# First layer in blocks of 512 tokens with all its weights resident, areas laid out by phase, and the GpSimd differences on VectorE

## Chip, cores and metric

One NeuronCore of a Trainium2 chip runs the kernel. The metric is the device time of one execution in microseconds (us), median of several runs. Five engines run side by side, each in the order of its own queue: PE (TensorE, the matmuls), DVE (VectorE), ACT (ScalarE), POOL (GpSimd) and SP, which here only issues DMAs.

## What is computed

Linear attention with a normalisation per head, then two feed-forward layers, all in fp32:

```python
kv = einsum('bhsd,bhse->bhde', k, v)                   # 8 batches, 8 heads, 576 tokens, head size 64
out = einsum('bhsd,bhde->bhse', q, kv)
x = out / sqrt(mean(out * out, axis=-1) + 1e-6) * g_norm   # (4608 tokens, 512)
h = x @ w_in                                           # layer one: (512, 2048)
x = (maximum(h, 0) + alpha * minimum(h, 0)) @ w_out    # (2048, 512)
return ((x @ w_a) * (x @ w_b)) @ w_out2                # layer two: (512, 1536) twice, (1536, 512)
```

## The kernel before

**Precision and products.** Every operand of the layers is split into a rounded high half (fp32r) and the rest, and a product is three matmuls (high by low, low by high, high by high). Each large product uses Strassen's scheme in Winograd's form on 2 x 2 quarters: seven sub-products instead of eight, paid for with additions and differences of quarters before and after. A sub-product has two slices of 128 rows, so it is six matmuls.

**Units.** A unit is the weight operand of one 256-column piece: its seven combinations, both halves, in one of eight places `w0` to `w7`. Weights arrive as 64-bit words. `to_float` (L229) turns them into floats with one ACT, four DVE and one POOL operation (L237 to L244); `combine` (L448) forms the four combinations S1 to S4 (L454) and splits them (ACT L461, DVE L463). A unit is made in one of two ways. With `fetch` and `direct` it is made straight from the input, as six of the eight `w_in` units are. With `convert` and `build`, floats are first written to DRAM (`wd`) and later read back when a place is free; then the combinations of L454 run on POOL.

**Stages.** Attention is 16 steps (two a batch): products of k and v (L278, L279), q by that (L295, L300), the norm on ACT and DVE, the scaling by it on POOL (L339), a transposition on PE (L349, L353), and a store of the result to `xd` in DRAM. The first four steps run ahead; the other twelve are put between products of layer one, two steps a piece of work, behind the first six pieces. Layer one and two then each have a stage of first products (`first`, PE line L540) and of second products (`second`, L616).

In `first` a piece is one block of 768 tokens by one pair of units. `X` loads the block into the place F0 (L485), forms differences of its quarters (`less`, L500) and splits the seven operands into `rops` (ACT L507, DVE L508). The differences of the first block may run on DVE; those of all later blocks are on POOL. Each sub-product is 384 wide and has a bank of PSUM for each unit; ACT copies it to H (L547) or DVE adds it (L550). Then layer one's activation follows (ACT L577 and L578, DVE L579), or the product of a and b in layer two (L582), and H is stored to `gd` in DRAM. H alternates between the places F1 and F2.

In `second` a block is 512 tokens; for each of 8 (layer one) or 6 (layer two) units it loads 256-wide quarters of `gd` into one of the places F0, F1, F2 (L597), forms four differences (L602: the first on POOL, three on DVE), splits them (ACT L608, DVE L609) into one of three parts of `rops` and adds 42 matmuls to seven banks. After the last unit ACT copies one bank (L625) and DVE adds the others (L629).

**Order.** Nothing is ordered by hand. `Plan.add` records each operation with its cost, priority and data it reads and writes; `Plan.order` (L113) is a list scheduler that places them on engines by these costs, and its order is the program's order on every engine. An operation waits for the older users of a place that it overwrites.

Priorities are due times: START for the first piece, URGENT for copies and additions of banks, `due` for conversions. The list V (L658) gives the sequence of blocks; six places hold units until attention ends, two more come from the memory that attention frees.

Of the kernel before, what the change touches and what calls it, by code (L numbers as in the profile page):

```python
# [24 lines left out]
NB1, NB2 = TOK // T1ST, TOK // T2ND  # L25
CH = 112
EPS = 1e-6
QN = 2
# [6 lines left out]
PAIR = 14 * 6 * (N1 + 32) / 2400  # L35
UNIT2 = 7 * 6 * (N2 + 32) / 2400
START, STEP = 50.0, 12.5
ATT = 30.0
NFIRST = 4
BUILD, CONVERT = 14.0, 10.0  # L40
# [112 lines left out]
def body(ctx: ExitStack, tc, kvm, kvt, qt, gn, w_in, alpha, w_o1, w_a, w_b, w_o2, outT):  # L153
# [19 lines left out]
    def in_dram(shape, name):  # L173
        t = dram.tile(shape, F32, name=name)
        return Buf(lambda: t)
# [16 lines left out]
    rops = pool.tile([P, 7 * 4 * N1], F32R, name="rops")  # L192
# [17 lines left out]
    def bank(tag, shape):  # L210
        return place(tag, shape, F32, psum)

    tenants = []

    def rop(lo, n):

        before = []
        for e in list(tenants):
            a, z, b = e
            if a < lo + n and lo < z:  # L220
                before += b.tasks
                if lo <= a and z <= lo + n:
                    tenants.remove(e)
        b = Buf(lambda: rops[:, lo:lo + n], before)
        tenants.append((lo, lo + n, b))
        return b

# [25 lines left out]
    class Step:  # L253
# [57 lines left out]
        def norm(self):  # L311
# [6 lines left out]
            for s in range(2):  # L318
                sq = place("T1", [P, NT, P])
# [22 lines left out]
        def tr(self, tags):  # L342
# [11 lines left out]
            y = [sb("y", [P, SEQ], 3) for _ in range(2)]  # L354
# [17 lines left out]
    def slot(key, shape, dt):  # L372
        old = plan.rings.get(key)
        b = Buf(lambda: (late[0] if key in SLOTS[6:] else pool).tile(shape, dt, tag=key, name=key),
                old.tasks if old else (attention if key in SLOTS[6:] else ()))
# [3 lines left out]
    class Unit:  # L379
# [57 lines left out]
        def build(self, key, prio):  # L437
# [5 lines left out]
            self.combine(prio, 1, "p")  # L443
# [27 lines left out]
    class X:  # L471


        def __init__(self, la, b):
            self.la, self.b = la, b
            self.x = place("F0", [P, 4, 2, N1])

        def load(self, prio):
            xf, t0, done = self.x, self.b * T1ST, 0
            src, size = (x2d, T2ND) if self.la else (xd, SEQ)  # L480
            while done < T1ST:
                p, o = divmod(t0 + done, size)
                m = min(T1ST - done, size - o)
                hs = [h for h in range(2) if done < (h + 1) * N1 and done + m > h * N1]
                dma(m * 2048, lambda done=done, m=m: xf.t.rearrange("p k h t -> p k (h t)")[:, :, done:done + m],  # L485
                    lambda p=p, o=o, m=m: src[p].t[:, :, o:o + m], prio, [(src[p], k) for k in range(4)],
                    [(xf, (r, h)) for r in range(2) for h in hs])
                done += m

        def operands(self, prio, engines="v", split_on="v"):  # L490
# [349 lines left out]
```

## Time and profile before

| What | Value |
|---|---|
| median of 3 runs (lowest, highest) | 1813.35 us (1812.14, 1814.52) |
| the profiled execution's own time | 1813.78 us |
| its span, first to last instruction | 1812.0 us |
| PE, DVE, ACT, POOL busy in the span | 92%, 74%, 48%, 33% |
| mean granted clock of PE | 0.962 |
| moved by DMA | 287.10 MB, 158 GB/s |

A row of the stretches has, after its bounds and length, the busy time of each engine and its number of instructions, the granted clock of PE as a share of full speed, and DMA's share and rate. A row of a group has the line, engine and operation, what it writes and reads, the count, the busy time and mean duration (ns), then the idle time ahead of it and what ended that. A waiting row has the waiting engine and line, what it waited for, the total in us, the times and the longest. A row with three durations gives the least, the median and the greatest in ns. In a timeline, start and length in us stand first and an idle time ahead, with its cause, in brackets.

### The profile page before, as it was taken

How to read it: one execution, taken by the hardware profiler on the slowest of the kernel's cores; microseconds unless marked ns; L12 is line 12 of the kernel's file. 1: busy time of each engine (PE TensorE's matmuls, PEld its weight loads, DVE VectorE, ACT ScalarE, POOL GpSimd, SP SyncE). 2: the span in 40 equal slices, each digit the busy share in tenths (PEclk: the TensorE clock that was granted, in tenths of full speed). 3: DMA queues.
4: the chain of work that ended last, by engine and by line, in shares of the span. 5: the costliest groups of instructions: out<-in, count | busy, mean ns of one | idle time of the engine just before them, and what ended most of it. 6: DMA issues, size and time to landing. Idle time of an engine off the chain costs nothing.

```text
span 1812.0 us, 28663 instructions
## 1 busy us (share of the span) xinstructions
PE 1662.9 (92%) x11132; PEld 1636.3 (90%) x11132; DVE 1349.3 (74%) x1794; ACT 864.9 (48%) x1223; POOL 593.2 (33%) x423
## 2 busy tenths in 40 slices
PE   5588968879899699999998999999999999999998
PEld 5487868879799599999998999999999999999998
DVE  5886755788867789889898767666785557778785
ACT  4466756767678433333334543444544334333332
POOL 2323224332334223433345723223633112222221
PEclk8798978989899899999999999999999999999999
DMA  8646866454534445455554333334353223444442
GB/s 247 226 139 214 257 221 196 150 195 159 204 140 167 164 158 163 158 159 166 174 190 156 128 134 134 122 124 152 137 174 130 105 87 120 131 143 138 149 132 93
DMA packets 174440, 287.10 MB, mean 158 GB/s; under 512 B 14304, under 2 KB 95200, under 8 KB 174304
## 3 DMA queue, kind: packets, MB, share of 16 engines
q1 hardware_dynamic: 174304, 285.28, 47.4%
q8 instruction: 87, 1.43, 0.3%
q14 instruction: 49, 0.40, 0.1%
HBM read 176.17 MB, written 109.05 MB: 157 GB/s over the span
## 4 chain that ended last, share of the span: by engine, by line
PE 68%; DVE 15%; issue 7%; ACT 5%; POOL 3%; DMA 1%; SPq 0%; DVEq 0%; ACTq 0%; POOLq 0%
PE b L540 42%; PE b L616 21%; ACT rops L608 2%; PE b L295 2%; DVE F L602 2%; DVE rops L609 2%; DVE rops L508 2%; POOL stg L454 1%; DVE F L579 1%; PE b L278 1%; DVE stg L239 1%; DVE F L550 1%; DVE w L463 1%; PE b L349 1%; POOL stg L244 1%
## 5 line engine op out<-in xcount | busy, mean ns | idle before, releaser
L540 PE MATMUL b<-rops,w 128*128 128x384 f32 x5040 | 916.1, 342 | 65.1 <-DVE rops L508 33.4
L540 PEld LDWEIGHTS b<-rops,w 128*128 128x128 f32 x5040 | 890.0, 192 | 79.7 <-DVE rops L508 34.9
L616 PE MATMUL b<-rops,w 128*128 128x256 f32 x5292 | 644.6, 285 | 27.8 <-DVE rops L609 22.6
L616 PEld LDWEIGHTS b<-rops,w 128*128 128x128 f32 x5292 | 639.2, 192 | 33.3 <-DVE rops L609 23.8
L608 ACT CAST rops<-F 128x1792 fp32r<-128x1792 f32 x126 | 211.6, 1694 | 409.5 <-DVE F L602 131.9
L547 ACT COPY F<-b 128x384 f32<-128x384 f32 x480 | 228.1, 478 | 353.3 <-PE b L540 346.3
L609 DVE TENSOR_TENSOR rops<-F,rops 128x1792 fp32r<-128x1792 f32 x126 | 264.9, 2116 | 98.4 <-ACT rops L608 97.3
L550 DVE TENSOR_TENSOR F<-F,b 128x384 f32<-128x384 f32 x360 | 194.6, 549 | 179.4 <-ACT F L547 85.8
L602 POOL TENSOR_TENSOR F<-F 128x256 f32<-128x256 f32 x126 | 148.0, 1178 | 395.4 <-DMA F<-gd 334.9
L244 POOL TENSOR_TENSOR stg<-stg 128x512 f32<-128x512 f32 x56 | 100.2, 1789 | 314.2 <-DVE stg L242 170.1
L602 DVE TENSOR_TENSOR F<-F 128x256 f32<-128x256 f32 x378 | 180.2, 504 | 8.3 <-DMA F<-gd 4.0
L508 DVE TENSOR_TENSOR rops<-F,rops 128x768 fp32r<-128x768 f32 x120 | 148.7, 1253 | 19.9 <-ACT rops L507 19.6
L454 POOL TENSOR_TENSOR stg<-stg 128x256 f32<-128x256 f32 x112 | 123.5, 1114 | 66.3 <-DMA stg<-wd 55.1
L579 DVE SCALAR_TENSOR_TENSOR F<-F,nal_sb,t 128x768 f32<-128x768 f32 x96 | 117.3, 1233 | 32.7 <-ACT F L578 32.2
L507 ACT CAST rops<-F 128x768 fp32r<-128x768 f32 x120 | 98.6, 836 | 23.5 <-POOL F L500 11.1
L500 POOL TENSOR_TENSOR F<-F 128x768 f32<-128x768 f32 x38 | 77.5, 2044 | 55.1 <-DVE rops L508 54.3
L577 ACT ACTIVATE t<-F 128x768 f32<-128x768 f32 x96 | 80.9, 847 | 21.8 <-DVE F L579 19.6
L463 DVE TENSOR_TENSOR w<-stg,w 128x1792 fp32r<-128x1792 f32 (+2 forms) x36 | 76.7, 2134 | 18.2 <-ACT w L461 18.1
L582 DVE TENSOR_TENSOR F<-F 128x768 f32<-128x768 f32 x72 | 80.5, 1125 | 13.0 <-ACT F L547 12.4
L578 ACT ACTIVATE F<-F 128x768 f32<-128x768 f32 x96 | 79.8, 844 | 0.6
L339 POOL TENSOR_TENSOR o<-o,sm 128x640 f32<-128x640 f32 x32 | 48.9, 1548 | 92.1 <-DVE sm L334 87.8
L500 POOL TENSOR_TENSOR T<-F 128x768 f32<-128x768 f32 x19 | 38.0, 1998 | 123.5 <-DMA F<-x2d 77.4
(64 smaller groups left out, 883.7 us busy)
## 6 DMA issues: line engine op xcount, KB each, us to landing
gd<-F SPq DMA_DIRECT2D x168, 384.0 KB, 2.8
F<-gd SPq DMA_DIRECT2D x252, 256.0 KB, 3.0
kvm<-in_kvm_dram SPq DMA_DIRECT2D x32, 448.0 KB, 5.4
wd<-stg SPq DMA_DIRECT2D x56, 256.0 KB, 2.0
stg<-in_w_o_dram SPq DMA_DIRECT2D x28, 512.0 KB, 4.7
stg<-wd SPq DMA_DIRECT2D x56, 256.0 KB, 3.5
F<-x2d SPq DMA_DIRECT2D x12, 1024.0 KB, 6.3
q<-in_qt_dram SPq DMA_DIRECT2D x32, 288.0 KB, 3.3
```

The source lines that it names most:

```text
L244: task("p", n, lambda: nc.gpsimd.tensor_add(out(), permute(f32(a())), permute(f32(u()))), prio, [A, U], [dst])
L454: sub(256, lambda e, o=o, f=f, a=a, b=b: getattr(e, f)(c.t[:, o], c.t[:, a], c.t[:, b]), prio, r, [(c, {S1: "S1", S2: "S2", S3: "S3", S4: ...
L500: sub(n, lambda e: e.tensor_sub(o[0](), a[0](), b[0]()), prio, a[1] + b[1], o[1], engines)
L508: sub(n, lambda e: e.tensor_sub(w(1), v(), f32(w(0))), prio, a[1] + [(c, 0)], [(c, 1)], split_on)
L540: nc.tensor.matmul(bk.t[:, 0:N1], w.h.t[:, a, i, kk, :], ct[:, b, kk, :], start=bool(new and kk == 0 and m == 0), stop=(kk == 1 and m == 2 ...
L547: task("a", N1, lambda: nc.scalar.copy(H.t[:, u, q], bk.t[:, 0:N1]), t - URGENT, [(bk, 0)], [(H, (u, q))])
L550: task("v", N1, lambda: nc.vector.tensor_add(H.t[:, u, q], H.t[:, u, q], bk.t[:, 0:N1]), t - URGENT, [(bk, 0), (H, (u, q))], [(H, (u, q))])
L579: task("v3", T1ST, lambda r=r, v=v, nal=nal: nc.vector.scalar_tensor_tensor(v(), v(), nal, r.t, ALU.mult, ALU.add), t, pv + [(r, 0)], pv)
L602: sub(N2, lambda e, o=o, a=a, c=c: e.tensor_sub(s.t[:, o[0]], s.t[:, a[0]], s.t[:, c[0]]), k - 9, [a[1], c[1]], [o[1]], on)
L608: task("a", 7 * N2, lambda: nc.scalar.copy(half(0), s.t[:, 0:7]), k - 7, reads, [(c, 0)])
L609: sub(7 * N2, lambda e: e.tensor_sub(half(1), s.t[:, 0:7], f32(half(0))), k - 7, reads + [(c, 0)], [(c, 1)], "v")
L616: nc.tensor.matmul(bk[i].t[:, m], unit.h.t[:, a, i, m, :], half(e)[:, i], start=bool(j == 0 and m == 0 and z == 0), stop=bool(j == n - 1 a ...
```

## The change

- Blocks of `first` in layer one are 512 tokens (256-wide sub-products, nine blocks, 36 pieces instead of 24); layer two keeps 768.
- All eight `w_in` units are fetched and made directly in the eight places and stay until the last block of the stage; all blocks take the four pairs in turn.
- Attention steps after the fourth come one to two pieces; the first four have due times 0, 8, 30 and 40. q has three buffers instead of two.
- The copies and additions of banks take both units in one operation (512 elements in layer one, 768 in layer two). X, Y and Z are one bank each in layer one (X alternating between two), two banks each in layer two.
- Fixed places F0 to F2 give way to ranges of two areas, `fa` and `rops`, and of two more, `rl` and `fl`, that exist from the end of attention. `second` rotates over four source places instead of three.
- All differences of operands and of `second`, and the combinations in `build`, run on DVE; POOL keeps one addition of `to_float` (L244 before) and the scaling in attention.
- The due times of conversions are spread between the stages' needs, and the loads of blocks come earlier.

```diff
-T1ST, N1 = 768, 384
+T1ST = (512, 768)
-QN = 2
+QN = 3
-START, STEP = 50.0, 12.5
-ATT = 30.0
+START = 40.0
+ATT = 20.0
+STEP_AT = [0, 8, 30, 40]
+FETCH_AT = [4, 12, 20, 25, 32, 36, 42, 48]
-    rops = pool.tile([P, 7 * 4 * N1], F32R, name="rops")
+    rops = pool.tile([P, 7168], F32R, name="rops")
+    fa = pool.tile([P, 7680], F32, name="fa")
...
-            self.combine(prio, 1, "p")
+            self.combine(prio)
...
-    def first(k, la, units, js, x):
+    def first(k, la, units, js, x, odd):
+        t1st, n1, pair = T1ST[la], T1ST[la] // 2, PAIR[la]
+        places = [((0, 1), (6, 7))[odd], (2, 3), (4, 5)] if la else [odd, 2, 3]
+        X_, Y_, Z_ = [bank(i, [P, 2, 256]) for i in places]
+        H = area("f", odd * 8 * n1, 8 * n1, (2, 4, n1))
...
-        def copy(u, q, bk, t):
-            task("a", N1, lambda: nc.scalar.copy(H.t[:, u, q], bk.t[:, 0:N1]), t - URGENT, [(bk, 0)], [(H, (u, q))])
+        def copy(q, bk):
+            task("a", 2 * n1, lambda: nc.scalar.copy(H.t[:, :, q], bk.t[:, :, 0:n1]), k + pos * dt - URGENT,
+                 [(bk, 0), (bk, 1)], [(H, (0, q)), (H, (1, q))])
...
+        prod(0, X_, 1)
+        copy(0, X_)
+        prod(2, Y_, 1)
+        copy(3, Y_)
+        prod(1, X_, 0)
+        copy(1, X_)
+        prod(4, Z_, 1)
+        add(0, Z_)
+        prod(3, X_, 0)
+        add(3, X_)
+        prod(5, Y_, 0)
+        add(1, Y_)
+        prod(6, X_, 0)
+        copy(2, X_)
...
+    SOURCE = [[("f", 4096), ("fl", 0), ("f", 0), ("f", 2048)], [("fl", 0), ("f", 0), ("f", 4096), ("f", 2048)]]
+    TURN = [[2, 0, 1], [0, 1, 2]]
...
-        for o, a, c, on in ((t3, b22, b12, "p"), (t1, b12, b11, "v"), (t2, b22, t1, "v"), (t4, b21, t2, "v")):
+        for o, a, c, on in ((t3, b22, b12, "v"), (t1, b12, b11, "v"), (t2, b22, t1, "v"), (t4, b21, t2, "v")):
-        c = rop((plan.counts.setdefault("gx", 0) % 3) * 14 * N2, 14 * N2)
+        c = rop(TURN[la][(b * n + j) % 3], 14 * N2)
...
-    V = [(0, 0, [0, 1, 2]), (0, 1, [0, 1, 2]), (0, 2, [0, 1, 2, 3]), (0, 0, [3]), (0, 3, [0, 1, 2, 3]), (0, 1, [3]),
-         (0, 4, [0, 1, 2, 3]), (0, 5, [0, 1, 2, 3])]
+    V = [(0, b, [0, 1, 2, 3]) for b in range(NB1[0])]
...
-            x.load(tn - 30)
-            x.operands(tn - 9, "p", "pv")
+            x.load(tn - 70)
+            x.operands(tn - 9)
```

PE's order around the later attention steps, before (L540 are products of layer one, L349 and L353 transpose a step, L295 and L300 are q's products of the next, L278 and L279 the k and v products of the one after):

```order
L540 MATMUL b_2120<-rops,w_530 128x384 x6
L349 MATMUL b_2131<-ident,o_109 128x112 x4
L295 MATMUL b_2139<-kvbd,q_2073 112x128 x4
L349 MATMUL b_2146<-ident,o_109 128x112 x4
L353 MATMUL b_2152<-ident,o_109 128x128 x2
L295 MATMUL b_2158<-kvbd,q_2079 112x128 x4
L300 MATMUL b_2164<-kvbd,q_2073 128x128
L300 MATMUL b_2164<-kvbd,q_2079 128x128
L278 MATMUL b_2171<-kvm_2092 128x128 x4
L279 MATMUL b_2171<-kvt_2100 128x128
L278 MATMUL b_2171<-kvm_2103 128x128 x4
L279 MATMUL b_2171<-kvt_2110 128x128
```

The next step's own matmuls follow these rows, again with no product between. At the like place of the changed kernel (L576 are its products, L380 and L384 the transposition of one step):

```order
L380 MATMUL banks<-ident,o_110 128x112 x8
L576 MATMUL banks<-rops,w_949 128x256 x6
L576 MATMUL banks<-rops,w_1124 128x256 x6
L576 MATMUL banks<-rops,w_1193 128x256 x6
L576 MATMUL banks<-rops,w_830 128x256 x6
L384 MATMUL banks<-ident,o_110 128x128 x2
```

Products of two pieces (the weights of pairs three and four) now stand between the matmuls of one step, and later steps are spread likewise.

DVE's order in `second` of layer one, before (L602 are differences, L609 low halves; F stands for the three places):

```order
L602 TENSOR_TENSOR F_6356<-F_6356 128x256 x3
L602 TENSOR_TENSOR F_6386<-F_6386 128x256
L609 TENSOR_TENSOR rops<-F_6289,rops 128x1792
L609 TENSOR_TENSOR rops<-F_6356,rops 128x1792
L602 TENSOR_TENSOR F_6386<-F_6386 128x256 x2
L609 TENSOR_TENSOR rops<-F_6386,rops 128x1792
```

Three differences belong to each low half; the fourth of each unit is in POOL's queue. The same place now (L652 are differences, L658 low halves; fa and fl hold the four source places, rl the third operand part):

```order
L658 TENSOR_TENSOR rl<-fl,rl 128x1792
L652 TENSOR_TENSOR fa<-fa 128x256 x3
L658 TENSOR_TENSOR rops<-fa,rops 128x1792
L652 TENSOR_TENSOR fa<-fa 128x256 x5
L658 TENSOR_TENSOR rops<-fa,rops 128x1792
L652 TENSOR_TENSOR fl<-fl 128x256 x3
```

Each low half now has four differences on DVE itself, and those of several units are interleaved ahead of it; POOL's queue holds none of them.

More of the change, by code (lines that the diff above doesn't have):

```diff
@@ L208, in sb, with bank, make, area @@
         return place(keys[i % len(keys)], shape, dt, pool)
[L210 to L218, printed above, removed]
+    banks = psum.tile([P, 8, 512], F32, name="banks")
+    def bank(which, shape):
+        which = [which] if isinstance(which, int) else list(which)
+        old = [plan.rings[f"ps{i}"] for i in which if f"ps{i}" in plan.rings]
+        lo, n = which[0], int(np.prod(shape[1:]))
+        def make():
+            if len(which) > 1:
+                return banks[:, lo:lo + len(which)]
+            t = banks[:, lo, 0:n]
+            return t.rearrange("p (a b) -> p a b", a=shape[1]) if len(shape) > 2 else t
+        b = Buf(make, [x for o in old for x in o.tasks])
+        for i in which:
+            plan.rings[f"ps{i}"] = b
+        return b
+    tenants = {"r": [], "f": [], "rl": [], "fl": []}
+    def area(kind, lo, n, shape=None):
+        before = list(attention) if len(kind) > 1 and not tenants[kind] else []
+        for e in list(tenants[kind]):
             a, z, b = e
@@ L557, in first, with go @@
[L557 to L566 removed]
+            c = x.c[i]
+            for u in range(2):
+                w = units[u]
+                def go(u=u, w=w):
+                    ct = c.t.rearrange("p (b k t) -> p b k t", b=2, k=2)
+                    for kk in range(2):
+                        for m, (a, b) in enumerate([(0, 1), (1, 0), (0, 0)]):
+                            nc.tensor.matmul(bk.t[:, u, 0:n1], w.h.t[:, a, i, kk, :], ct[:, b, kk, :],
+                                             start=bool(new and kk == 0 and m == 0 and (la or u == 0)), stop=(kk == 1 and m == 2),
+                                             skip_group_check=True)
+                end = task("t", 6 * (n1 + 32), go, k + pos * dt, w.parts(i) + [(c, 0), (c, 1)] + (
+                    [(bk, 0)] if u and new and not la else []), [(bk, u)])
+                pos += 1
@@ L743, in body @@
             units = (pairs1, us2)[la][j]
-            end = first(t, la, units, [2 * j, 2 * j + 1] if la == 0 else [j], x)
+            end = first(t, la, units, [2 * j, 2 * j + 1] if la == 0 else [j], x,
+                        pi % 2)
         else:
@@ L748, in body @@
             if fst:
-                bk = [bank(f"b{i}", [P, 2, N2]) for i in range(7)]
+                bk = [bank(i, [P, 2, N2]) for i in range(7)]
             end = second(t, la, b, j, n, units[0], bk)
```

231 lines of the change are left out of this document (113 added, 118 removed).

## Prediction

> **What bounds the kernel now.** I read the busy times by stage first (stretches cut where the first matmul of a stage, or a gap, begins), then what PE waited for in them, then the longest unbroken runs of matmuls in the chain that ended last.
>
> ```profile
> core 0: us, PE busy (x) PEld busy (x) DVE busy (x) ACT busy (x) POOL busy (x), PEclk, DMA share, GB/s
> 0.00:72.80 72.80, 35.75 (x200) 33.34 (x200) 46.05 (x89) 32.75 (x59) 23.59 (x24) 0.79 0.82 249
> 72.80:150.00 77.20, 65.99 (x412) 64.16 (x413) 60.18 (x103) 48.82 (x83) 15.97 (x11) 0.93 0.55 179
> ...
> 245.00:284.00 39.00, 21.26 (x111) 18.27 (x112) 19.35 (x37) 11.31 (x22) 14.79 (x10) 0.68 0.68 214
> ...
> 400.00:590.00 190.00, 180.97 (x1015) 179.08 (x1013) 147.06 (x179) 146.63 (x228) 67.94 (x49) 0.97 0.49 175
> 590.00:621.00 31.00, 13.46 (x92) 13.09 (x93) 28.09 (x30) 16.27 (x15) 10.49 (x9) 0.80 0.45 153
> 621.00:986.00 365.00, 358.92 (x2939) 354.56 (x2938) 312.63 (x401) 132.20 (x98) 129.03 (x93) 0.99 0.52 167
> 986.00:1004.00 18.00, 11.47 (x47) 9.96 (x46) 15.35 (x13) 7.67 (x8) 17.22 (x11) 0.81 0.41 131
> 1004.00:1530.00 526.00, 521.94 (x2988) 518.54 (x2987) 355.85 (x454) 229.18 (x397) 171.05 (x120) 1.00 0.37 128
> 1530.00:1545.00 15.00, 11.18 (x81) 10.78 (x79) 13.72 (x18) 5.58 (x4) 5.63 (x5) 0.89 0.49 163
> 1545.00:1812.00 267.00, 261.02 (x2184) 260.82 (x2184) 202.57 (x260) 87.80 (x59) 61.85 (x49) 1.00 0.41 131
> ```
>
> The stages are: attention start to 72.8; first products of layer one with the rest of attention to 590; second products of layer one to 986; layer two's first products to 1530, and its second products. The chain gives what a stage costs when nothing waits:
>
> ```profile
> 238.75 0.89 PE b L278 x8
> 485.61 99.14 PE b L540 x570
> 1545.35 259.60 PE b L616 x2172
> ```
>
> A 384-wide matmul takes 99.14/570 = 173.9 ns, a 256-wide one 259.60/2172 = 119.5 ns, an attention one 0.89/8 = 0.111 us, so an attention step of 50 matmuls 5.6 us. Layer two is nearly full: (3024 - 47) x 0.1739 = 517.7 of 526 us, and 2268 x 0.1195 = 271 of 282. Idle or slowly clocked time lies elsewhere. To 590, 2016 x 0.1739 = 350.6 and 16 x 5.6 = 89.6 leave 590 - 440 = 150 us. From 590 to 986, 3024 x 0.1195 = 361.4 of 396 leaves 35. From 986 to 1004, 47 x 0.1739 = 8.2 of 18 leaves 10. So the change can win only in layer one and at the seams. What PE waited for, from 72 to 590, then from 590 to 1004:
>
> ```profile
> PE b L540 <- DVE rops L508: 30.8, 12, 8.3
> PE b L540 <- DVE F L550: 21.0, 12, 4.9
> PE b L349 <- POOL o L339: 10.6, 3, 5.5
> ```
> ```profile
> PE b L616 <- DVE rops L609: 18.4, 4, 12.4
> ```
>
> And PE's own timeline where its clock is lowest:
>
> ```profile
> 249.17 2.29 PE L540 MATMUL b<-rops,w 128*128 128x384 f32 x6 [4.94 <-DVE F L550]
> ...
> 266.43 1.01 PE L349 MATMUL b<-ident,o 112*128 112x112 f32 x4 [4.67 <-POOL o L339]
> ...
> 283.02 1.01 PE L349 MATMUL b<-ident,o 112*128 112x112 f32 x4 [5.51 <-POOL o L339]
> ```
>
> Between 251.5 and 283.8 there is no product: attention steps stand one behind another in PE's order, each taking about 16.6 us (266.43 to 283.02) through DVE, ACT and POOL for 5.6 us of PE.
>
> **Part by part.** *Blocks of 512.* 3024 x 0.1195 - 2016 x 0.1739 = +10.8 us on the full engine. The two widths give 54.4 ns for 128 columns and 10.8 ns per matmul that no width pays for. The Trainium skill (TensorE: Matmul & The Clock Gate, Back-to-back issue gap) gives columns at 2.4 GHz plus about 2.5 ns; by that this term would be an estimated +2.6 us. The trace disagrees (10.8 ns), and I keep +10.8.
>
> *The start, all eight units resident.* Products may start after batch 0 instead of batches 0 and 1, but pairs 2 to 4 are needed at once, so DVE sets the pace until unit eight is ready. Its prices:
>
> ```profile
> L463 DVE TENSOR_TENSOR w<-stg,w 128x1792 fp32r<-128x1792 f32 (+2 forms) x36 | 76.7, 2134 | 18.2 <-ACT w L461 18.1
> L242 DVE SCALAR_TENSOR_TENSOR stg<-stg 128x512 f32<-128x512 uint32 x56 | 42.2, 753 | 0.3
> L239 DVE SCALAR_TENSOR_TENSOR stg<-stg 128x512 int32<-128x512 int32 x56 | 41.4, 739 | 0.5
> L241 DVE TENSOR_SCALAR stg<-stg 128x512 int32<-128x512 int32 x56 | 32.1, 573 | 0.1
> L238 DVE TENSOR_SCALAR stg<-stg 128x512 int32<-128x512 int32 x56 | 23.9, 427 | 5.9 <-ACT stg L237 5.8
> L454 DVE TENSOR_TENSOR stg<-stg 128x256 f32<-128x256 f32 x24 | 12.4, 518 | 0.8 <-POOL stg L244 0.7
> L322 DVE TENSOR_REDUCE sm<-T 128x10 f32<-128x640 f32 x32 | 26.1, 814 | 28.5 <-ACT T L320 18.9 <-issue 9.4
> L330 DVE TENSOR_TENSOR sm<-sm 128x20 f32<-128x20 f32 x16 | 7.5, 470 | 0.1
> L629 DVE TENSOR_TENSOR y<-y,b 128x512 f32<-128x512 f32 x54 | 35.2, 679 | 0.0
> L579 DVE SCALAR_TENSOR_TENSOR F<-F,nal_sb,t 128x768 f32<-128x768 f32 x96 | 117.3, 1233 | 32.7 <-ACT F L578 32.2
> ```
>
> A unit is 2 x (0.427 + 0.739 + 0.573 + 0.753) + 4 x 0.518 + 2.134 = 9.2 us, eight are 73.5. By the order, seven attention steps (estimate 4 us each: two reductions of 0.814 and eight small operations of at most 0.47), nine bank additions (0.679), ten activations (1233 x 512/768 = 0.82) and eleven operand operations (about 0.7) stand ahead of its end: 123 us in all. Before, DVE was busy 46.05 + 60.18 = 106 of the 139 us from 10.8 (its first work) to 150, 76%. At that pace the unit is ready at 10.8 + 162 = 173, at full pace at 134; I take nine tenths, 148, since POOL's operand differences are gone and q has a third buffer. By then three of 36 pieces are done.
>
> *The rest of the first stage.* 33 pieces x 84 x 0.1195 = 331 and nine steps x 5.6 = 50: 382 us. Attention is now spread at one step to two pieces (the order in the change shows products between its matmuls), so its 16 us chain lies beside 20 us of products. From 400 to 590, with no attention, 190 us held 1015 matmuls x 0.174 = 176, 7% lost. I take 9%, as H (the output of a piece) turns over in a shorter time: 382 + 34 = 416. The stage ends at 148 + 416 = 564 instead of 590: **-26 us** (the +10.8 is inside), with -45 to +10 as ends.
>
> *No GpSimd differences.* 126 of second, 78 (now 84) of operands and 112 of the weights go to DVE.
>
> ```profile
> L602 DVE TENSOR_TENSOR F<-F x378: 408/420/1515, 544.3 to 1791.6; 128x256 f32<-128x256 f32 x189
> L602 POOL TENSOR_TENSOR F<-F x126: 727/910/2627, 540.5 to 1788.3; 128x256 f32<-128x256 f32 x126
> L609 DVE TENSOR_TENSOR rops<-F,rops x126: 2012/2026/3121, 587.8 to 1793.9; 128x1792 fp32r<-128x1792 f32 x126
> ...
> L602 DVE TENSOR_TENSOR F<-F 128x256 f32<-128x256 f32 x378 | 180.2, 504 | 8.3 <-DMA F<-gd 4.0
> L609 DVE TENSOR_TENSOR rops<-F,rops 128x1792 fp32r<-128x1792 f32 x126 | 264.9, 2116 | 98.4 <-ACT rops L608 97.3
> ```
>
> The same DVE difference takes 420 ns at the median, 504 in the mean and 1515 at worst, and POOL's runs from 727 to 2627: they hold each other up. The Trainium skill (SBUF — State Buffer, Who interferes with whom) says that a DVE instruction with two SBUF inputs and a GpSimd one that reads SBUF exclude each other, the later waiting for all of the earlier; the spread above agrees. At the medians a unit of second costs DVE 4 x 0.42 + 2.026 + 7 x 0.679/8 = 4.3 us, at the means 4.73, in 5.02 us of PE (42 x 0.1195). Layer one's also hold twelve conversion halves, 12 x 2.5/72 = 0.42 us a unit: 4.72 or 5.15. I take the medians, since POOL keeps only the conversions' addition there. DVE then follows PE closely, at 94%. At the seams unit 0 finds its own operand place (rl) free, so the 12.4 us wait goes; eight builds of 4 x 0.42 + 2.03 = 3.7 us come late next, beside 35 us of products. Idle time 35 becomes 18: **-17** (ends -27 and +9). The seam into layer two, where POOL's differences held the weights, 10 becomes 5: **-5**.
>
> *Operations over both units.* Copies fall from 480 to 288, additions from 360 to 216, and fixed shares are saved on ACT and DVE that have slack in layer two; on PE's path it gives nothing. It lengthens each hand-over of a bank (next part): I take +7 in layer two's first products, ends 0 and +40. The last seam and the tail: **-3**. Four source places and the earlier loads only deepen the prefetch; a load that waits on SP holds up the stores and loads queued behind it there, but the plan places loads 16 us ahead of their products, three units of 5.02; I cost it at nothing (up to +5 if SP's order blocks).
>
> Sum: -26 - 17 - 5 + 7 - 3 = -44 on the span of 1812.0, 1768. The profiled execution took 1813.78, 1.8 more than its span and 0.4 above the median 1813.35: 1768 + 1.8 - 0.4 = 1769.
>
> **Rivals.** *Hand-overs of a bank (slower).* Prod 0 of both units, then the copy of the bank, then prod 1 into the same bank: only two products lie between. That is 12 x 0.1195 = 1.43 us in layer one for a copy of 0.58 or an addition of 0.68, and 2.09 us in layer two for some 0.8 to 0.95.
>
> ```profile
> L625 ACT COPY y<-b 128x512 f32<-128x512 f32 x12 | 7.0, 580 | 11.0 <-PE b L616 11.0
> L577 ACT ACTIVATE t<-F 128x768 f32<-128x768 f32 x96 | 80.9, 847 | 21.8 <-DVE F L579 19.6 <-DVE F L550 1.2
> ```
>
> Behind one activation (estimate 0.63 for 512 from 847 for 768) or a 2.03 us difference the bank comes late. There are 3 x 72 = 216 such hand-overs. At 0.4 us each the time is 1769 + 86 = 1855; from 44/216 = 0.2 us on average it is slower than before. For it: 21.0 us waited on L550 with single-unit additions. Against: the order puts products of the next piece between, and 1004 to 1530 lost only 8 us with the same distance.
>
> *DVE gets no relief.* With the means, second of layer one is DVE's: 72 x (5.15 - 5.02) = 9 more, its idle time stays (+17), the start keeps 76% (+25): 1820, or 1805 if only half of it holds: about no change. For it: DVE was busy 312.63/365 = 86% of that stage already. Against: POOL's own work of 129 us in that stage mostly goes.
>
> *A clean first stage (faster).* Unit eight at full pace (134, -14) and 4% lost after it (-19), and layer two without its +7: 1729, with seams at half again 1720. For it: 400 to 590 lost 7% with the contention; against: a DVE that never waited has no row.
>
> **How the numbers follow.** Forecast 0.60, hand-overs 0.15, no relief 0.13, clean 0.12. The forecast's own range is 1735 to 1800. The range runs from 1712, just below the clean case, to 1832, beyond no relief and into mild hand-overs, leaving out most of the hand-over case. About 0.2% (3.6 us) can be told from no change. Faster: 0.60 less 0.01, 0.12 and 0.04 of no relief, 0.75; same 0.06 (no relief, and the forecast's edge); slower 0.19 (hand-overs and 0.04).
>
> **What would show it.** Right: the first product near 50 to 60; unit eight's low half near 148; the first of second near 560; no stretch like 251 to 284 without products; DVE's 256-wide difference near 420 in the mean; second of layer one within 380 us. Wrong: PE waiting for the bank copies or additions by more than 40 us in all; the difference staying at 500; DVE at 97% or more from 570 to 950 with PE waiting for its low halves.

## The result, and the profile after

The changed kernel takes 1751.19 us (median of 4 runs, 1749.41 to 1753.7), the kernel before 1812.74 us beside it: a ratio of 0.9661, 95% interval 0.9645 to 0.9678. The forecast was 1769 with a range of 1712 to 1832. The profiled execution took 1751.36 us, its span is 1749.6 us, and the granted clock averages 0.974 instead of 0.962. One execution among all those below, the fourth of e5, ran at a granted clock of 0.836 and took 1852.62 us; the other three of e5 lie between 1759.87 and 1762.28.

Line numbers have moved. In the kernel after, L576 is a product of a first stage and L665 one of a second; L584 copies banks out and L589 adds them; L617 to L619 are the activation; L652 are the differences of a second unit, L657 and L658 its operand (cast and low half); L534, L541 and L542 are the differences, casts and low halves of a block's operands; L484 and L493 are the differences and the low half of a weight build.

Busy times by stage of the changed kernel, cut where a stage or a gap begins (columns as in the first table of the prediction):

```profile
core 0: us, PE busy (x) PEld busy (x) DVE busy (x) ACT busy (x) POOL busy (x), PEclk, DMA share, GB/s
0.00:58.60 58.60, 28.45 (x141) 26.12 (x141) 33.90 (x65) 23.20 (x41) 18.98 (x18) 0.79 0.83 256
58.60:144.00 85.40, 62.23 (x474) 59.67 (x474) 78.73 (x135) 51.38 (x90) 31.50 (x19) 0.90 0.62 192
144.00:355.00 211.00, 208.60 (x1758) 208.30 (x1759) 159.26 (x271) 164.20 (x311) 35.85 (x22) 0.99 0.65 213
355.00:440.00 85.00, 75.42 (x591) 74.61 (x590) 67.34 (x107) 59.80 (x114) 17.91 (x12) 0.92 0.55 184
440.00:533.00 93.00, 89.28 (x733) 88.26 (x732) 71.61 (x111) 68.93 (x119) 2.93 (x2) 1.00 0.48 161
533.00:579.00 46.00, 28.52 (x223) 27.12 (x223) 43.00 (x66) 31.08 (x40) 0.00 (x0) 0.87 0.49 164
579.00:932.00 353.00, 352.92 (x2938) 352.61 (x2938) 311.57 (x462) 135.85 (x98) 28.06 (x12) 0.99 0.50 162
932.00:975.00 43.00, 42.86 (x248) 42.54 (x247) 38.66 (x50) 20.09 (x24) 3.25 (x2) 1.00 0.42 141
975.00:1455.00 480.00, 480.00 (x2768) 480.00 (x2767) 356.44 (x431) 193.85 (x238) 36.38 (x22) 1.00 0.41 137
1455.00:1482.00 27.00, 15.64 (x100) 15.23 (x99) 15.64 (x26) 7.54 (x5) 0.00 (x0) 0.81 0.44 146
1482.00:1749.60 267.60, 261.90 (x2184) 261.69 (x2183) 205.30 (x307) 87.34 (x58) 0.00 (x0) 0.99 0.41 129
```

From 579 to 1455 next to nothing is lost any more: neither in the second products of layer one, nor at the seam into layer two (18 us at a clock of 0.81 before), nor in layer two's first products. What is left lies mostly before 144, in 355 to 440, and at two seams, 533 to 579 and 1455 to 1482. PE's own waits from 58 to 600, then its timeline at both seams:

```profile
PE banks L665 <- DVE rops L658: 15.7, 2, 14.5
PE banks L576 <- ACT fa L584: 14.3, 9, 3.5
PE banks L380 <- POOL o L370: 8.5, 2, 8.3
PE banks L326 <- DVE kvbd L315: 7.5, 2, 5.1
PE banks L576 <- DVE w L493: 5.3, 4, 1.9
PE banks L576 <- DVE rops L542: 4.0, 1, 4.0
PE banks L576 <- DVE fa L589: 2.6, 3, 1.3
```
```profile
578.34 7.82 PE L665 MATMUL banks<-rops,w 128*128 128x256 f32 x42 [14.52 <-DVE rops L658]
...
1465.73 7.84 PE L665 MATMUL banks<-rops,w 128*128 128x256 f32 x42 [3.24 <-DVE rops L658]
1481.69 6.76 PE L665 MATMUL banks<-rl,w 128*128 128x256 f32 x42 [8.12 <-DVE rl L658]
```

At each seam the longest wait is for the low half of an operand of the second products, that of their third unit. I put the stages beside the forecast. The boundaries are the first product of layer two (986.1 before, 932.2 after) and the last of layer two's first products (1529.5 and 1458.2):

| part | before | after | difference | forecast |
|---|---|---|---|---|
| start to the first product of layer two | 986.1 | 932.2 | -53.9 | -43 (-26 and -17) |
| to the end of layer two's first products | 543.4 | 526.0 | -17.4 | +2 (-5 and +7) |
| the rest | 282.5 | 291.4 | +8.9 | -3 |

So 18 us more were gained than forecast (62 against 44), and the parts are off in both directions.

### The profile page after: what moved, and what is told of

Same layout as the page of the kernel before. It is cut to its first block, busy times and chain, and to the rows that moved or that the text cites. A ratio compares the mean times of both kernels' runs of the same rounds, so it can differ in the third digit from the quotient of the medians.

```text
span 1749.6 us, 30530 instructions
## 1 busy us (share of the span) xinstructions
PE 1645.8 (94%) x12140; PEld 1636.2 (94%) x12140; DVE 1381.5 (79%) x2023; ACT 843.3 (48%) x1134; POOL 174.9 (10%) x109
## 4 chain that ended last, share of the span: by engine, by line
PE 85%; DVE 8%; ACT 3%; issue 2%; DMA 1%; POOL 1%; DVEq 0%; SPq 0%; ACTq 0%; POOLq 0%
PE banks L576 45%; PE banks L665 36%; PE banks L326 2%; PE banks L309 1%; DVE fa L619 1%; DVE w L493 1%; DVE fa L589 1%; ACT fa L617 1%; POOL o L370 1%; DVE rops L658 1%; DVE rops L542 1%; ACT fa L618 1%; PE banks L380 0%; DVE stg L484 0%; ACT fa L584 0%
## 5 line engine op out<-in xcount | busy, mean ns | idle before, releaser
L576 PE MATMUL banks<-rops,w 128*128 128x256 f32 (+1 forms) x4752 | 702.1, 305 | 26.3 <-ACT fa L584 14.3
L576 PEld LDWEIGHTS banks<-rops,w 128*128 128x128 f32 x4752 | 676.1, 193 | 30.5 <-ACT fa L584 16.6
L665 PE MATMUL banks<-rops,w 128*128 128x256 f32 x3528 | 436.4, 285 | 19.0 <-DVE rops L658 18.9
L665 PEld LDWEIGHTS banks<-rops,w 128*128 128x128 f32 x3528 | 431.6, 194 | 20.0 <-DVE rops L658 19.8
L584 ACT COPY fa<-banks 128x512 f32<-128x512 f32 (+1 forms) x288 | 195.7, 692 | 283.1 <-PE banks L576 280.4
L589 DVE TENSOR_TENSOR fa<-fa,banks 128x512 f32<-128x512 f32 (+1 forms) x216 | 176.2, 818 | 128.9 <-PE banks L576 85.1
L576 PE MATMUL banks<-rl,w 128*128 128x384 f32 x1296 | 238.8, 336 | 0.1
L576 PEld LDWEIGHTS banks<-rl,w 128*128 128x128 f32 x1296 | 225.8, 188 | 0.5 <-DVE fa L589 0.5
L665 PE MATMUL banks<-rl,w 128*128 128x256 f32 x1764 | 217.8, 281 | 8.8 <-DVE rl L658 8.1
L665 PEld LDWEIGHTS banks<-rl,w 128*128 128x128 f32 x1764 | 213.0, 189 | 9.5 <-DVE rl L658 8.3
L657 ACT CAST rops<-fa 128x1792 fp32r<-128x1792 f32 x62 | 104.9, 1695 | 199.7 <-PE banks L665 120.4
L658 DVE TENSOR_TENSOR rops<-fa,rops 128x1792 fp32r<-128x1792 f32 x62 | 127.4, 2059 | 42.7 <-ACT rops L657 42.6
L652 DVE TENSOR_TENSOR fa<-fa 128x256 f32<-128x256 f32 x376 | 146.7, 429 | 3.6 <-DMA fa<-gd 2.0
L619 DVE SCALAR_TENSOR_TENSOR fa<-fa,nal_sb 128x512 f32<-128x512 f32 x144 | 120.5, 845 | 34.8 <-ACT fa L618 34.1
L617 ACT ACTIVATE fa<-fa 128x512 f32<-128x512 f32 x144 | 89.6, 631 | 50.8 <-DVE fa L619 25.1
L542 DVE TENSOR_TENSOR rops<-fa,rops 128x512 fp32r<-128x512 f32 (+1 forms) x99 | 87.1, 887 | 25.8 <-ACT rops L541 25.5
L657 ACT CAST rl<-fa 128x1792 fp32r<-128x1792 f32 x32 | 54.1, 1690 | 97.9 <-DVE fa L652 29.7
L618 ACT ACTIVATE fa<-fa 128x512 f32<-128x512 f32 x144 | 89.4, 631 | 1.3
L541 ACT CAST rops<-fa 128x512 fp32r<-128x512 f32 (+1 forms) x99 | 68.2, 697 | 29.0 <-PE banks L576 20.2
L658 DVE TENSOR_TENSOR rl<-fa,rl 128x1792 fp32r<-128x1792 f32 x32 | 65.8, 2056 | 18.6 <-ACT rl L657 18.5
```

The lines of the kernel that those rows point to most:

```text
L542: sub(n, lambda e: e.tensor_sub(w(1), v(), f32(w(0))), prio, a[1] + [(c, 0)], [(c, 1)], "v")
L576: nc.tensor.matmul(bk.t[:, u, 0:n1], w.h.t[:, a, i, kk, :], ct[:, b, kk, :], start=bool(new and kk == 0 and m == 0 and (la or u == 0)), st ...
L584: task("a", 2 * n1, lambda: nc.scalar.copy(H.t[:, :, q], bk.t[:, :, 0:n1]), k + pos * dt - URGENT, [(bk, 0), (bk, 1)], [(H, (0, q)), (H, ( ...
L589: task("v", 2 * n1, lambda: nc.vector.tensor_add(H.t[:, :, q], H.t[:, :, q], bk.t[:, :, 0:n1]), k + pos * dt - URGENT, [(bk, 0), (bk, 1)] ...
L617: task("a", t1st, lambda r=r, v=v: nc.scalar.activation(r.t, v(), AF.Relu), t, pv, [(r, 0)])
L618: task("a", t1st, lambda v=v: nc.scalar.activation(v(), v(), AF.Relu, scale=-1.0), t, pv, pv)
```

## The experiments

All medians are of four runs. The three middle columns, from the profiled execution of each, are the starts of the first product of the second products of layer one, of layer two, and of layer two's second products.

| run | median us | second, layer one | layer two | second, layer two | span |
|---|---|---|---|---|---|
| before | 1812.7 | 590.5 | 986.1 | 1529.4 | 1812.0 |
| after | 1751.2 | 533.3 | 932.2 | 1455.2 | 1749.6 |
| e1, all GpSimd differences back | 1773.7 | 545.0 | 951.9 | 1477.9 | 1772.8 |
| e2, those of the second products | 1752.3 | 535.4 | 936.3 | 1459.6 | 1753.6 |
| e10, those of the builds | 1753.0 | 530.9 | 930.2 | 1455.8 | 1750.4 |
| e12, those of the operands | 1769.0 | 541.6 | 940.9 | 1468.8 | 1762.8 |
| e3, before without them | 1795.6 | 590.2 | 978.4 | 1515.4 | 1796.9 |
| e4, before, attention spread | 1822.4 | 603.4 | 997.5 | 1541.9 | 1826.0 |
| e5, attention clumped | 1762.2 | 542.8 | 942.0 | 1465.0 | 1758.1 |
| e6, banks by unit | 1773.4 | 567.8 | 959.1 | 1483.8 | 1771.9 |
| e8, layer two in 512 | 1763.4 | 532.6 | 931.4 | 1482.0 | 1762.1 |
| e9, repeat of after | 1750.1 | 532.4 | 931.2 | 1454.3 | 1748.6 |
| e11, three places | 1751.7 | 531.8 | 940.0 | 1463.4 | 1749.2 |
| f1, early places | 1741.4 | 523.9 | 923.3 | 1446.6 | 1738.9 |

My theory after the result: the differences that left GpSimd and the spread attention made the gain. The rival: the order, the residency and the places made it, and the rest was hidden either way.

**Is it the GpSimd differences?** First all of them back in the changed kernel, and all of them out of the kernel before.

```
-        for o, a, c, on in ((t3, b22, b12, "v"), (t1, b12, b11, "v"), ...
+        for o, a, c, on in ((t3, b22, b12, "p"), (t1, b12, b11, "v"), ...
...
-            x.operands(tn - 9)
+            x.operands(tn - 9, "p", "pv")
...
-            self.combine(prio)
+            self.combine(prio, 1, "p")
```

The second edit names the engines of a block's differences and of its low halves, the third those of a build's differences.

> The changed kernel with all its GpSimd differences put back: one of four in each unit of the second products, the operand differences of every block after the first, and the four of each weight build that is loaded from memory. Theory (GpSimd's differences held DVE up, and taking them away filled the second products of layer one and the seam into layer two): 1751 goes up by 20 to 35 us, to about 1780; the 256-wide difference on DVE is back near 500 ns in the mean, PE again loses 10 to 18 us between 579 and 932 and about 10 us at the seam into layer two. Rival (the order of the work, four source places and earlier loads did it, and GpSimd had hidden its part beside DVE): within 6 us of 1751, and the second products of layer one stay dense.

Measured: 1773.66 us (1772.08 to 1774.79), +22.5, as the theory said. But the place was only half as expected: 11.7 us are lost before the first of the second products, 8.0 in that stage, 3.5 behind it.

The mirror image, in the kernel before (the same three edits, backwards):

> The kernel before with nothing but the GpSimd differences moved to DVE (second products, operands of later blocks, weight builds). Theory (GpSimd's differences held DVE up): 1813 falls by 15 to 30 us, to about 1790; the 256-wide difference falls from 504 to about 430 ns in the mean and the stage of the second products of layer one (590 to 986) gets 10 to 15 us shorter. Rival (DVE is the bound there, and the differences only pay with the new order): 1813 within 5 us, or up to 15 us slower, with DVE at 95% between 621 and 986.

Measured: 1795.56 us (1793.45 to 1798.66), -17.1, ratio 0.9901 (0.9881 to 0.9922). The stage of the second products is 7.4 us shorter (388.2 instead of 395.6), less than the 10 to 15 expected, layer two's first products and the seam ahead of them 6.2; the 256-wide difference falls from 504 to 436 ns:

```profile
L602 DVE TENSOR_TENSOR F<-F 128x256 f32<-128x256 f32 x504 | 194.4, 436 | 4.9 <-DMA F<-gd 2.2
```

Nothing is gained in the first stage there. So GpSimd's differences cost 17 us in the kernel before and 22 in the changed one, though not in the same stages, and they are worth taking away without anything else of the change. Then one group at a time:

> The changed kernel with only one of four differences of each unit of the second products back on GpSimd. The run with all of them back was 22 us slower, by its stages 12 us to the first product of the second, 8 us in the second products of layer one, 3 after that. Theory (each group costs where it stands): 8 to 11 us slower, 1759 to 1762, with the first stage unchanged within 2 us. Rival (the operand differences and the weight builds made all of it, and DVE has room in the second products): within 4 us of 1751.

Measured: 1752.31 us (1748.41 to 1755.34): +1. The rival holds, though the mechanism is there. The differences by shape in this kernel (e2), and in the changed kernel:

```profile
L652 DVE TENSOR_TENSOR fa<-fa 128x256 f32<-128x256 f32 x282 | 137.5, 508 | 4.1 <-DMA fa<-gd 1.2
L652 POOL TENSOR_TENSOR fa<-fa 128x256 f32<-128x256 f32 x94 | 126.1, 1342 | 379.7 <-DMA fa<-gd 299.2 <-DVE fa L619 43.8 <-DVE stg L484 18.0
```
```profile
L652 DVE TENSOR_TENSOR fa<-fa 128x256 f32<-128x256 f32 x376 | 146.7, 429 | 3.6 <-DMA fa<-gd 2.0
...
L619 DVE SCALAR_TENSOR_TENSOR fa<-fa,nal_sb 128x512 f32<-128x512 f32 x144 | 120.5, 845 | 34.8 <-ACT fa L618 34.1
...
L584 ACT COPY fa<-banks 128x512 f32<-128x512 f32 x144 | 80.8, 584 | 38.8 <-PE banks L576 36.1 <-DVE stg L272 1.2
L589 DVE TENSOR_TENSOR fa<-fa,banks 128x512 f32<-128x512 f32 x108 | 73.5, 684 | 39.8 <-PE banks L576 33.7 <-ACT fa L618 3.6 <-ACT fa L584 1.3
L542 DVE TENSOR_TENSOR rops<-fa,rops 128x512 fp32r<-128x512 f32 x63 | 47.3, 760 | 10.6 <-ACT rops L541 10.4
L534 DVE TENSOR_TENSOR fa<-fa 128x512 f32<-128x512 f32 x36 | 28.9, 808 | 0.1
```

With one in four on GpSimd the others take 508 ns in the mean instead of 429, the slow-down seen before the change. Three at 508 are 1.52 us of DVE a unit, four at 429 are 1.72: GpSimd takes one of four away, and DVE saves half of one. The stage itself is 2 us longer (400.9 instead of 398.9). So the contention is measured, and hardly on the path; that DVE has room there (88% busy in the changed kernel) and makes operands ahead of PE is the likely reason, and e11 below bears it out.

> The changed kernel with only the weight builds' four differences back on GpSimd (26 builds). All groups back cost 22 us, the one of the second products alone 1. Theory (a build on GpSimd takes some 4 us instead of 1.7 and comes late at the seam, and its operations hold DVE up): 5 to 10 us slower, 1756 to 1761, all of it between 533 and 932, the first stage to its end unchanged within 2 us; the operand differences then made the other 12 of the first stage. Rival (the loss needs all groups at once, since only together they fill DVE): within 3 us of 1751.

Measured: 1752.96 us (1752.04 to 1757.28): +2. The rival holds; the builds alone cost nothing that I can tell.

> The changed kernel with only the operand differences of every block after the first back on GpSimd (the four 512- or 768-wide ones on GpSimd alone, the seven low halves on GpSimd or DVE by the plan). All three groups back cost 22 us, the second products' alone 1, the builds' alone 2. Theory (the three add up, and this one made the rest in the first stage, where a block's operands are due within two pieces of 10 us): 14 to 20 us slower, 1765 to 1771, the first of the second products 10 us or more later. Rival (only all three together hold DVE up enough, none costs by itself): within 5 us of 1751.

Measured: 1769.04 us (1764.61 to 1770.41), +18; its profiled execution is the fastest of the four, so its stages show less of it (8 us to the first of the second products, 5 in layer two's first). The sizes of the theory hold: the three groups alone come to 18 + 1 + 2 = 21 of the 22.5, and the operands are nearly all of it. The groups in e12, against the rows above:

```profile
L619 DVE SCALAR_TENSOR_TENSOR fa<-fa,nal_sb 128x512 f32<-128x512 f32 x144 | 129.3, 907 | 48.1 <-ACT fa L618 47.6
...
L542 DVE TENSOR_TENSOR rops<-fa,rops 128x512 fp32r<-128x512 f32 x63 | 50.4, 813 | 11.6 <-ACT rops L541 11.6
L534 POOL TENSOR_TENSOR fa<-fa 128x512 f32<-128x512 f32 x32 | 49.1, 1536 | 141.0 <-DVE rops L542 75.6 <-DMA fa<-xd 29.3 <-issue 21.3
```

A difference of a block takes 1536 ns instead of 808, and meanwhile the activation (845 to 907 ns) and the low halves (760 to 813) on DVE get longer. What PE waited for in e12, from 58 to 600:

```profile
PE banks L326 <- DVE kvbd L315: 12.2, 3, 4.5
PE banks L576 <- DVE fa L589: 8.5, 7, 2.4
PE banks L576 <- DVE rops L542: 1.4, 1, 1.4
```

PE did not wait longer for the low halves of the blocks' operands (1.4 us, 4.0 in the changed kernel). It waited longer for DVE's additions of banks (8.5 instead of 2.6) and for DVE's copies in attention (12.2 instead of 7.5). By these waits, what comes late in the first stage is DVE's other work, and not the block's operands that the theory named.

**Is it the spread of attention?** In the kernel before, over nine pieces instead of six; in the changed kernel, clumped as before.

```
-                for _ in range(2):
+                for _ in range(2 if len(pieces) % 3 == 1 else 1):
```

> The kernel before with its twelve later attention steps over the first nine pieces of products instead of the first six (two at every third piece, one at the others). Theory (attention steps one behind another leave PE without products, about 20 us of it between 245 and 284): 10 to 20 us faster, 1795 to 1803, and no stretch of over 20 us without products. Rival (the start and DVE's work for the first units set that stage, so the loss only moves): within 5 us of 1813.

Measured: 1822.43 us (1821.89 to 1827.8), 10 us slower, ratio 1.0055 (1.0034 to 1.0075). The theory has the wrong sign, and the loss did not merely move, as the rival said, but grew. The hole from 245 to 284 is filled (43.47 of 45 us busy from 245 to 290, 27.26 before), and a larger one opens. PE's timeline there:

```profile
316.24 1.01 PE L349 MATMUL b<-ident,o 112*128 112x112 f32 x4 [8.62 <-POOL o L339]
...
331.60 1.01 PE L349 MATMUL b<-ident,o 112*128 112x112 f32 x4 [7.78 <-POOL o L339]
...
350.52 0.69 PE L540 MATMUL b<-rops,w 128*128 128x384 f32 x1 [16.27 <-ACT w L461]
```

The first six units have run out of products, and units seven and eight take places that come free only when attention has ended; spreading attention holds them back, and PE waits 16.3 us for the first of them. So in the kernel before, spreading attention does not pay while two units wait for attention's memory; whether residency alone would change that was not tried there.

```
-            if nstep < 2 * NBAT and len(pieces) >= 3 + 2 * (nstep - NFIRST):
-                at_time[nstep] = len(pieces) - 1
-                nstep += 1
-                t += 5.4
+            if ps is not None and nstep < 2 * NBAT:
+                for _ in range(2):
+                    at_time[nstep] = len(pieces) - 1
+                    nstep += 1
+                    t += 5.4
```

> The changed kernel with its twelve later attention steps two to a piece at the first six pieces, as before the change, instead of one to two pieces. Theory (spreading hides the 16 us chain of a step): 12 to 25 us slower, 1763 to 1776, with stretches without products again. Rival (in the changed kernel DVE's work for the weight units is the bound of the start, and attention finds room beside it anywhere): within 5 us of 1751.

Measured: 1762.18 us, ratio 0.9716 (0.9693 to 0.9739) against the changed kernel's 0.9661: 11 us slower, just short of the theory's 12 to 25. The waits for GpSimd's scaling of an attention output rise from 8.5 to 18.1 us:

```profile
PE banks L380 <- POOL o L370: 18.1, 6, 9.3
```

**Operations over both units.** Each copy (shown) and each addition cut in two, one for each unit:

```
-            task("a", 2 * n1, lambda: nc.scalar.copy(H.t[:, :, q], bk.t[:, :, 0:n1]), ...
+            for u in range(2):
+                task("a", n1, lambda u=u: nc.scalar.copy(H.t[:, u, q], bk.t[:, u, 0:n1]), ...
```

> The changed kernel with each copy and addition of a bank cut in two, one for each unit, as before the change (288 copies and 216 additions become 576 and 432, half as wide). Theory (the longer hand-over of a bank over both units costs nothing, since products of the next piece stand between): no gain, within 6 us of 1751, or slower by up to 10 us in the first stage by the fixed share of the added operations on DVE. Rival (the 17 us that PE waits for copies and additions of banks in the first stage are the longer hand-overs): 8 to 15 us faster.

Measured: 1773.36 us (1772.05 to 1774.44), 22 us slower: more than either theory had. The copies and additions of layer one in e6, to be held against L584 and L589 at 512 above:

```profile
L585 ACT COPY fa<-banks 128x256 f32<-128x256 f32 x288 | 94.2, 379 | 99.1 <-PE banks L576 97.7 <-DVE fa L591 1.1
...
L591 DVE TENSOR_TENSOR fa<-fa,banks 128x256 f32<-128x256 f32 x216 | 84.3, 416 | 64.0 <-PE banks L576 48.6 <-ACT fa L585 9.2 <-issue 2.1
```

Two halves take 758 ns for 584 and 832 for 684. Neighbours overlap a little, so the busy time rises by less than these: ACT 94.2 us for 80.8, DVE 84.3 for 73.5. By the table the first of the second products comes 34.5 us later, some of which returns at the seams. In layer two's first products it changes nothing (524.8 us from the first to the last of them, against 526.0 with six matmuls of the second products among them), so the longer hand-over that I charged there costs nothing either.

**The width of a block.**

```
-T1ST = (512, 768)
+T1ST = (512, 512)
```

> The changed kernel with layer two's first products in blocks of 512 tokens as well. Theory (a matmul has 10.8 ns that no width pays for): 4536 x 0.1195 - 3024 x 0.1739 = +16.2 us, 1767, and the stage of 523 us becomes about 539. Rival (a fixed share of about 2.5 ns for each of the 1512 added matmuls): +4 us, 1755.

Measured: 1763.37 us (1761.8 to 1767.88), +12. A dense stretch of e8 gives the price itself:

```profile
976.00:1446.00 470.00, 469.06 (x3905) 468.45 (x3904) 351.22 (x548) 196.67 (x327) 34.09 (x22) 1.00 0.40 135
```

or 120.4 ns a matmul of 256, against 480/2768 = 173.4 ns of 384 above. From the first product of layer two to the end of its first products (1477.9 in e8) it takes 546.5 us instead of 526.0: 20.5 more, rather above the 16.2 of the theory and far from the rival's 4. The total rose by less, because what follows is 7 us shorter: PE waits 5.0 us for low halves at the last seam instead of 11.4.

**The start.** The differences of the eight resident units on either engine:

> The changed kernel with the four 256-wide differences of each of the eight resident units given to DVE or GpSimd, whichever the plan finds free first. Theory (the start from 58 to 144 is DVE's, busy 78.73 of 85.4 us there): a third of 32 differences of 0.5 us leave DVE, 3 to 6 us faster, 1746 to 1748. Rival (a GpSimd difference holds the DVE ones up by as much as it takes over): the same or up to 8 us slower, with L484 on DVE above 553 ns in the mean in that stretch.

Nothing was learned of that: the plan gave all of them to DVE, and each engine's order is that of the changed kernel. Its 1750.13 us (1748.88 to 1754.74) is a second reading of 1751.

**Source places.** Three instead of four, with the GpSimd difference of e2 (its edit is not repeated here):

```
+    SOURCE = [[("f", 4096), ("fl", 0), ("f", 0)], [("fl", 0), ("f", 0), ("f", 4096)]]
```

> The changed kernel with three source places for the second products instead of four, and one of four differences of each unit on GpSimd, as before the change; the same with four places took 1752. Theory (the fourth place is what hid the GpSimd difference and the loads, and made the stage of the second products dense): 8 to 15 us slower than 1752, with waits for low halves between 579 and 932. Rival (three places are enough, as the prediction had it): within 4 us of 1752.

Measured: 1751.65 us (1748.6 to 1753.4), no difference in the whole, but not because nothing happens. The stage of the second products of layer one takes 408.2 us instead of the 400.9 of e2, with waits spread over it:

```profile
579.00:932.00 353.00, 344.32 (x2854) 341.00 (x2854) 309.19 (x387) 129.73 (x91) 99.53 (x76) 1.00 0.49 156
```

and layer two's second products are as much shorter, since PE waits 4.4 us at the last seam instead of the 12.3 of e2. With the GpSimd difference, then, the fourth place is worth 7 us in layer one and costs 8 at the last seam. By the layout it lies there under the outputs of both last pieces, but how that costs time is told by the queues. ACT and DVE of the changed kernel at the last seam (e2 has the same order):

```profile
1468.13 0.76 DVE L652 TENSOR_TENSOR fa<-fa 128x256 f32<-128x256 f32 x2 [0.20 <-DMA fa<-gd]
1473.61 1.69 ACT L657 CAST rops<-fl 128x1792 fp32r<-128x1792 f32 x1 [9.99 <-PE banks L665]
1475.33 2.02 DVE L658 TENSOR_TENSOR rops<-fl,rops 128x1792 fp32r<-128x1792 f32 x1 [6.43 <-ACT rops L657]
1477.27 2.43 DVE L652 TENSOR_TENSOR fa<-fa 128x256 f32<-128x256 f32 x7
1479.62 2.02 DVE L658 TENSOR_TENSOR rl<-fa,rl 128x1792 fp32r<-128x1792 f32 x1
```

The third unit (rl) had its data by 1468.1 and three of its four differences by 1468.9. The fourth stands in DVE's queue behind the low half of the fifth unit (rops<-fl). That waits for ACT's cast of the same unit, and the cast waits until PE has finished the second unit, whose part of `rops` it overwrites. PE finished it at 1473.6 and then waited 8.1 us for the third unit. With one difference, cast and low half left (0.42, 1.69 and 2.02 us), that unit could have been ready at about 1473, an estimate from these rows: the wait is the order of the queues, not a place that came free too late. In e11 the fourth unit has the early place fl and a free part of `rops`, nothing of the kind stands ahead of the third, and PE waits 0.2 us for it.

A version of its own was made for the places: the first units of each second stage get source places that the last piece's output does not hold (the edit is shown in part).

```
+    SOURCE = [[("fl", 2048), ("fl", 0), ("f", 4096), ("f", 2048)],
+              [("fl", 2112), ("f", 0), ("f", 2048), ("f", 4608)]]
+    SLOT = [[4, 6, 5, 0, 3, 1, 2], [None, 1, 0, 3, 2, 4, 5]]
-    TURN = [[2, 0, 1], [0, 1, 2]]
+    TURN = [[2, 1, 0], [0, 1, 2]]
...
-        H = area("f", odd * 8 * n1, 8 * n1, (2, 4, n1))
+        H = area("f", 1536 + odd * 3072 if la else (1 - odd) * 2048, 8 * n1, (2, 4, n1))
```

> The changed kernel laid out anew so that the first three units of each stage of second products find source places that no output of the last pieces holds (two places in the memory that attention leaves, X of layer two ahead of its outputs, operand places in the order of their last use). Theory (at both seams PE waited, 14.5 us for one low half at 578 and 8.1 and 3.2 us after 1465, because a source place came free only with the last outputs): 10 to 20 us faster, 1731 to 1741. Rival (at the first of these seams DVE is full, 43 of 46 us, with eight builds of 3.7 us, so only the last seam gets shorter): 3 to 8 us faster, 1743 to 1748.

Measured: 1741.4 us (1740.69 to 1742.31), ratio to the kernel before 0.9599 (0.9585 to 0.9614): 10 us faster than the change, the near end of the theory, and the fastest of all. In f1 L583 and L674 are PE's first and second products, L591 copies banks, L661, L666 and L667 are the differences, casts and low halves of a unit. PE's waits from 530 to 1000, its timeline at the last seam, and two rows of ACT and DVE there:

```profile
PE banks L674 <- DVE rl L667: 5.7, 1, 5.7
PE banks L583 <- ACT fa L591: 3.0, 2, 2.8
PE banks L674 <- DVE rops L667: 0.3, 1, 0.3
```
```profile
1457.47 7.93 PE L674 MATMUL banks<-rops,w 128*128 128x256 f32 x42 [3.58 <-DVE rops L667]
1475.16 12.70 PE L674 MATMUL banks<-rops,w 128*128 128x256 f32 x84 [4.81 <-DVE rops L667]
```
```profile
1465.48 1.69 ACT L666 CAST rops<-fl 128x1792 fp32r<-128x1792 f32 x1 [8.54 <-PE banks L674]
1467.21 2.03 DVE L667 TENSOR_TENSOR rops<-fl,rops 128x1792 fp32r<-128x1792 f32 x1 [5.93 <-ACT rops L666]
```

The first seam's wait fell from 14.5 to 5.7 us and layer two starts 8.9 us earlier; the last seam's fell from 11.4 to 8.4 only. There the fifth unit's cast and low half still stand in the way, now ahead of the fourth unit (the wait of 4.81). An order without them was not tried. Three places in layer two alone, as in e11, were not tried with it.

## Why the prediction was right, and where it was not

*The direction, and the likeliest case.* Faster held. The gain was 62 us instead of 44, beyond the likeliest case's middle and inside its own range of 1735 to 1800. Part of that is luck: several terms were off, in both directions. No run takes the residency or the earlier loads alone out of the changed kernel, so how much of the 62 us is theirs stays open.

*Blocks of 512, +10.8.* Right in kind, rather small: by the stages of e8 and after, 546.5/4536 = 120.5 and 526.0/3024 = 173.9 ns, it is 3024 x 0.1205 - 2016 x 0.1739 = +14. The estimate of +2.6 beside it should read +2.5 (1008 matmuls more), and e8 shows that price to be far too small here.

*The start.* The first product came at 58.6 (forecast 50 to 60), the low half of unit eight was ready at 149.9 (148; the one at 143.9 is unit seven's), and from 58.6 to 144 DVE was busy 78.73 of 85.4 us, 92% (nine tenths). Right, though the differences of the start on another engine remain untried.

*The rest of the first stage.* Forecast 416 us at 9% lost, to 564. The last product came at 555.7. The 405.8 us from 149.9 hold 2754 first and 36 second products at 0.1195 and 418 attention matmuls at 0.111, 380 us, so 6% was lost. From last product to last product (592.5 before) the stage gained 37 us where I had 26. The reason given held in part: spreading attention is worth 11 us in the changed kernel (e5) and costs 10 in the kernel before (e4); 8 us more are the operand differences (e12).

*No GpSimd differences, -17 and -5.* About the right size, 22 and 17 us (e1, e3), at the wrong place. That POOL's differences in the second products slow DVE's is true (508 against 429 ns) and worth 1 us by itself in the changed kernel (e2). It is the operand differences that cost, 18 us (e12), most of it in the first stage, for which I had put down nothing apart from the start. From the last product of the first stage to the first of layer two the time did fall by 17 us (393.6 to 376.5). But 4 us of that are 30 matmuls of the second products that now run earlier (0.1195 each), and by e1 only 8 us of that stage are GpSimd's differences, by e2 2 us those that I meant, so that the number is in good part luck. DVE's share from 579 to 932 is 88% where I had 94%. The second products are dense rather than losing 10 us; the fourth source place is part of that, worth 7 us where a GpSimd difference stands beside it (e11).

*Four source places, "I cost it at nothing".* Wrong in both directions, 7 us gained and 8 lost (e11, both with a GpSimd difference).

*Operations over both units, "on PE's path it gives nothing", and +7 for the hand-overs.* Both wrong. Cutting them costs 22 us, all of it by the end of layer one's first stage (e6). The fixed shares that come back there, 13 us on ACT and 11 on DVE, are measured; that PE loses more than either because ACT and DVE then fall behind it is argued. The hand-overs cost nothing in layer two: 2768 matmuls stand in 480.00 us without a gap.

*The seam into the second products, "the 12.4 us wait goes".* It stayed, as 14.5 us, now for the third unit. I looked at the operand place of the first unit and not at the source place of the third, whose load was issued only at 563.0, behind the last pieces' stores. DVE was full as well (43.00 of 46 us): from 563.1 to the end of that low half at 578.3 it has no gap over 0.7 us, and two low halves of builds and one of the fifth unit stand in between. Given early places, 5.7 us are left (f1), for the fourth unit; DVE is nearly as full there (40.91 us from 533 to 579), so the builds that I named as next are likely, but no run tells them apart from the places.

*The last seam, -3.* It was +8.9. PE waited 11.4 us there instead of 4.2, and 8.1 of the 11.4 are the order on ACT and DVE that the rows with e11 show.

*The rivals.* Hand-overs: excluded by layer two's dense stage, and in layer one PE waited 14.3 us for copies and 2.6 for additions, not 86. No relief: excluded by e1 and e3 (half of its 51 us would have been 1795, not the 1805 that I wrote). A clean first stage: of its 33 us there some 10 came (406 us for the rest of the stage instead of 416, no earlier unit eight), and its layer two without the +7 came in full. The 17.4 us that layer two's first part gained are 6 from the differences (e3); the other 11, in banks that alternate, earlier loads or the new places, were not taken apart.

## What to carry to other kernels

When a stage is cut into smaller blocks, count the small operations around the matmuls as well: their fixed share can cost more than that of the matmuls, and one operation over both units pays it back. A second engine's help is priced by what it does to the first engine's operations, and stage by stage: here the same help cost 1 us in one stage and most of 18 in others. At a seam between stages, ask for every buffer that the next stage's first units use, sources as well as operands, who held it last, and then what stands ahead of those units in each engine's queue.

## What the runs showed of the hardware

A 256-wide difference on DVE rose from 429 to 508 ns in the mean when GpSimd ran one in four beside it (1342 ns each), so that DVE saved 0.2 us a unit instead of 0.43. This agrees with the rule of the Trainium skill (SBUF — State Buffer, Who interferes with whom) that the prediction drew on; that it cost only 2 us of that stage (e2) was not expected. A copy of 512 columns of one bank, 256 of each unit, took 584 ns against 379 for 256, an addition 684 against 416. And a matmul's price beyond its columns came out at 120.5 - 2 x (173.9 - 120.5) = 14 ns from two stages nearly without a gap, against 10.8 from the chain before.
